# Tiles 6 and 7 turned by moves and VectorE, regrouping by pairs through the DRAM, ScalarE normalising tiles 8 to 15

## The chip, the cores and the metric

The kernel runs on one core of a Trainium2 chip. The metric is the device time in microseconds (us) of one execution; lower is better.

## The reference, cut to what matters

`x` is 2048 tokens of 512 features, all float32. It is layer-normalised to `xn`; a linear-attention block and a two-layer block with a squared ReLU both read `xn`, and their results are added to `x`.

```python
xn  = (x - mean(x)) / sqrt(var(x) + 1e-5)
q, k, v = split(xn @ wqkv)                     # 32 heads of 16
phi = lambda t: where(t > 0, t + 1, exp(t)) + 1e-6
kv  = sum over tokens of phi(k)^T v            # per head
z   = sum over tokens of phi(k)
o   = (phi(q) @ kv) / (phi(q) . z + 1e-6)
out = x + o @ wo + relu(xn @ w1 + b1)**2 @ w2 + b2
```

## The kernel before, in words

The tokens are 16 tiles of 128, in blocks of TB = 4 tiles. Every matrix product is made of float32r products of a high and a low part: ScalarE copies the high part ("high", L292, or `copy`, L108), and VectorE or GpSimd makes the rest ("low", L295, or L116).

The part that matters here is the loop over tiles, L617 to L653. Iteration i, called **step i** below, issues on TensorE `project(i)` (L335, 12 matmuls into the PSUM bank `pk`: the keys of tile i) and `kx(i - 1)` (L354, 12 matmuls that add phi(k)^T xn of the tile before to four banks `kx`). So TensorE alternates 12 `pk` and 12 `kx` matmuls. `project(i)` needs the normalised tile with features on the partitions, in high and low parts. There are two ways to turn a tile:

- **By TensorE** (`turned_pe`, L271), tiles 0 to 7: four transposes (L276) into a bank `pt`; then ScalarE takes the high part, VectorE the low part, both from PSUM, and ScalarE copies the turned tile once more to SBUF (`keep_t`, L297) from where it is stored to DRAM (`xTd`, L302). In step i they turn tile i + 1, between `project(i)` and `kx(i - 1)`.
- **By moves and VectorE** (`turn`, L259), tiles 8 to 15: normalised tiles are written in a permuted order, 16 DMAs of 64 KB per four tiles (`regroup`, L245) move them from SBUF to SBUF so that 32 x 32 blocks stand right, and one VectorE transpose (L261) turns a tile. TensorE has no part in it.

VectorE computes mean and variance (`measure`, L213, L214), ScalarE a first inverse root (`roots`, L224, L225), VectorE refines it (L233 to L235) and normalises (L241). Both stand in step 2 to 7 for the tiles listed in `ahead` (L613): two tiles a step, out of order, (4, 8, 9) first. `phi` is ScalarE relu and exp (L326, L328) and VectorE's L330; `parts` makes the high part of phi(k) on ScalarE (L108) and the low part on VectorE (L343). `tokens` makes high (ScalarE) and low (GpSimd, L116) parts of the tile itself for `kx`. `pieces` (L607) takes the weights for later (`wq`, `wo`, `wv`) through ScalarE and VectorE, two a step from step 8 on; `fetch` loads them, at most three ahead.

The order on each engine is the order in which the program is written; there is no scheduler. All DMAs are issued by SyncE (SP), in order, and an SP instruction that waits holds up all DMAs behind it. [...] `regroup` only puts DMAs on the list `moves`; `move(n)` (L254) issues n of them, 16 a step before step 7 and 8 from then on.

After the loop come the queries, the attention and the two-layer block, twice eight tiles; nothing there is changed, except that `regroup_q` uses the old `regroup` under a new name.

## Time and profile before

| | |
|---|---|
| median of 3 runs | 423.33 us (423.31 to 423.94) |
| the profiled execution's own time | 423.45 us |
| its span in the profile | 421.7 us |
| TensorE matmuls busy | 416.7 us (99%) |
| VectorE, ScalarE, GpSimd busy | 298.4, 249.0, 28.5 us |
| granted TensorE clock | 1.0 |
| the tile loop of steps 3 to 15 on TensorE | 23.17 to 95.82 us of the span |

The span is counted from the first profiled instruction to the last; the execution's own time is 1.75 us more. Times of an instruction are from the span's start. TensorE's matmuls overlap in their pipeline, so the distance of their starts counts and not the length of one. The chain of waits follows the work that ended last backwards; where it lists only TensorE pieces without a gap, TensorE waited for nobody.

### The profile page before, as it was taken

The numbers are of one execution on the slowest core, as the hardware profiler recorded it, in microseconds if no ns is written. First come the engines' busy times: TensorE is split into PE (matmuls) and PEld (weight loads), VectorE is DVE, ScalarE is ACT, GpSimd is POOL, SyncE is SP. The second block draws the span as 40 slices with busy tenths as digits, with TensorE's granted clock in tenths as the row PEclk, the third lists the DMA queues.
The fourth block names the chain that finished last, engine by engine and source line by source line (L and its number), as shares of the span: only waits on it lengthen the run. The fifth ranks groups of instructions, "written<-read, shape, count | busy, mean of one in ns | idle before, by whom it ended". The sixth has DMA issues, their size and how long they took to land.

```text
span 421.7 us, 5377 instructions
## 1 busy us (share of the span) xinstructions
PE 416.7 (99%) x1868; PEld 344.9 (82%) x1868; DVE 298.4 (71%) x538; ACT 249.0 (59%) x445; POOL 28.5 (7%) x50
## 2 busy tenths in 40 slices
PE   8999999999999999999999999999999999999996
PEld 7788888888887888888888888888888888888885
DVE  6897788954678887777579376586977668577253
ACT  5866657645467777566466353666667665556140
POOL 3241222230000000000000000000000000000000
PEclk9999999999999999999999999999999999999999
DMA  7862347000412221546026652501120654024602
GB/s 230 284 186 75 101 108 222 21 0 3 112 50 66 85 87 39 188 88 174 0 64 195 185 201 82 139 0 50 51 75 25 200 100 151 1 89 92 163 0 99
DMA packets 42754, 43.02 MB, mean 102 GB/s; under 512 B 5828, under 2 KB 28612, under 8 KB 42472
## 3 DMA queue, kind: packets, MB, share of 16 engines
q1 hardware_dynamic: 42728, 42.69, 35.0%
q8 instruction: 14, 0.23, 0.2%
q14 instruction: 12, 0.10, 0.1%
HBM read 30.09 MB, written 6.29 MB: 86 GB/s over the span
## 4 chain that ended last, share of the span: by engine, by line
PE 98%; DVE 1%; DMA 1%; ACT 0%; issue 0%
PE acc L127 38%; PE b L427 23%; PE kx L354 10%; PE pk L335 10%; PE pq L335 10%; PE pz L127 1%; PE b L127 1%; PE pkv L737 1%; PE pt L276 1%; DMA x<-in_A_x_dram 1%; PE pm L127 1%; PE end L127 0%; DVE st L213 0%; DVE xp L241 0%; DVE res L867 0%; ACT xs1h L292 0%
## 5 line engine op out<-in xcount | busy, mean ns | idle before, releaser
L127 PE MATMUL acc<-w2r,s 128*128 128x512 f32 x498 | 116.6, 389 | 0.0
L127 PEld LDWEIGHTS acc<-w2r,s 128*128 128x128 f32 x498 | 93.5, 188 | 19.6
L427 PE MATMUL b<-T,aop 128*128 128x512 f32 x240 | 59.6, 389 | 0.0
L427 PEld LDWEIGHTS b<-T,aop 128*128 128x128 f32 x240 | 45.0, 188 | 9.4
L354 PE MATMUL kx<-pk,tok 128*128 128x512 f32 x192 | 47.1, 394 | 0.0
L354 PEld LDWEIGHTS kx<-pk,tok 128*128 128x128 f32 x192 | 35.4, 188 | 7.9 <-DVE pk L343 0.6
L127 PE MATMUL acc<-mh,aTsr 128*128 128x512 f32 x96 | 30.3, 390 | 0.0
L108 ACT ACTIVATE w2r<-r 128x512 fp32r<-128x512 f32 x32 | 20.0, 625 | 13.5 <-PE acc L127 11.0
L119 DVE TENSOR_TENSOR w2r<-r,w2r 128x512 fp32r<-128x512 f32 x32 | 21.9, 685 | 7.3 <-ACT w2r L108 6.4
L427 PE MATMUL b<-xs0h,aop 128*128 128x512 f32 x80 | 26.4, 391 | 0.0
L116 POOL TENSOR_TENSOR tok<-xp,tok 128x512 fp32r<-128x512 f32 x16 | 22.4, 1405 | 53.7 <-ACT tok L108 53.7
L116 DVE TENSOR_TENSOR s<-c,s 128x512 fp32r<-128x512 f32 x20 | 13.8, 692 | 16.7 <-ACT s L108 16.7
L330 DVE SCALAR_TENSOR_TENSOR q<-pq,q 128x512 f32<-128x512 f32 x16 | 11.0, 689 | 17.0 <-ACT q L328 17.0
L108 ACT ACTIVATE aop<-S 128x512 fp32r<-128x512 f32 x20 | 12.6, 629 | 14.6 <-DVE S L666 9.4
L127 PEld LDWEIGHTS acc<-mh,aTsr 128*128 128x128 f32 x96 | 18.0, 188 | 3.8
L198 POOL MEMSET r<- 32x512 f32 x3 | 1.6, 522 | 278.3 <-DVE w2r L119 278.2
L326 ACT ACTIVATE q<-pq 128x512 f32<-128x512 f32 x16 | 9.5, 591 | 18.0 <-PE pq L335 18.0
L867 DVE TENSOR_TENSOR res<-acc,res 128x512 f32<-128x512 f32 x16 | 11.0, 691 | 12.6 <-PE acc L127 12.6
L326 ACT ACTIVATE k<-pk 128x512 f32<-128x512 f32 x16 | 9.5, 595 | 16.9 <-PE pk L335 16.8
L127 PE MATMUL acc<-ml,aTsr 128*128 128x512 f32 x48 | 18.7, 390 | 0.0
L427 PEld LDWEIGHTS b<-xs0h,aop 128*128 128x128 f32 x80 | 15.0, 188 | 3.4 <-ACT rz L415 0.3
L261 DVE STREAM_TRANSPOSE at<-g 128x512 f32<-128x512 f32 x16 | 10.5, 690 | 8.5 <-DMA g<-q 8.5
(187 smaller groups left out, 835.7 us busy)
## 6 DMA issues: line engine op xcount, KB each, us to landing
r<-in_B_w_dram SPq DMA_DIRECT2D x49, 256.0 KB, 3.2
res<-in_A_x_dram SPq DMA_DIRECT2D x8, 512.0 KB, 6.2
g<-q SPq DMA_DIRECT2D x64, 64.0 KB, 2.1
out_dram<-res SPq DMA_DIRECT2D x15, 256.0 KB, 2.1
x<-in_A_x_dram SPq DMA_DIRECT2D x5, 512.0 KB, 6.3
xTd<-t SPq DMA_DIRECT2D x8, 256.0 KB, 3.5
rq<-in_A_wqkv_dram SPq DMA_DIRECT2D x8, 256.0 KB, 6.0
xg<-xp SPq DMA_DIRECT2D x32, 64.0 KB, 2.0
```

The costliest lines, as they stand in the source:

```text
L108: nc.scalar.activation(o, i, AF.Copy, bias=bias)
L116: ENG[el].tensor_tensor(out=l, in0=src, in1=f32(h), op=OP.subtract)
L119: nc.vector.tensor_tensor(out=l, in0=src, in1=f32(h), op=OP.subtract)
L127: nc.tensor.matmul(ps, lhsT=a[u], rhs=b[v], start=first and n == 0, stop=last and n == 2)
L261: nc.vector.transpose(o.rearrange("p j (r t) -> p r j t", r=NJ), G.rearrange("p r (j c) -> p r j c", j=NJ))
L276: nc.tensor.transpose(t[k][:, at:at + P], xp[i][:, j * P:(j + 1) * P], ident)
L326: nc.scalar.activation(p, ps, AF.Relu, scale=-1.0)
L330: nc.vector.scalar_tensor_tensor(p, ps, 0.0, p, op0=OP.max, op1=OP.add)
L335: nc.tensor.matmul(ps, lhsT=cols(i)[u][:, j, slot(i)], rhs=w[v][:, j, :], start=first and n == 0, stop=last and n == len(steps) - 1)
L354: nc.tensor.matmul(kxp[c], lhsT=tok[i][:, u, c * P:(c + 1) * P], rhs=pk[i][:, v], start=i == 0 and (u, v) == first, stop=i == NT - 1 and ( ...
L427: nc.tensor.matmul(ps, lhsT=a[u][:, j * P:(j + 1) * P], rhs=b[v][:, j, :], start=first and j == 0 and n == 0, stop=last and j == 1 and n == 2,
L867: nc.vector.tensor_tensor(out=r[:, a:z], in0=ps, in1=r[:, a:z], op=OP.add)
```

## The change

`NDVE` = 6 is the first tile that is turned by moves and VectorE, instead of `NPE` = 8, which stays the first tile whose turned form is kept in SBUF. Tiles 6 and 7 are still normalised by VectorE and still stored to `xTd`, from the buffer that VectorE's transpose writes. Tiles 8 to 15 are normalised by ScalarE: one ACTIVATE with a scale and a bias of one number per partition, after one more tiny VectorE operation on the statistics.

`regroup` now works on a pair of tiles, (6, 7), (8, 9), ... (14, 15): one DMA writes the pair (512 KB) to a DRAM tile `via`, and four DMAs of 128 KB read it back regrouped. The four are issued by `move()`, which now stands at the head of each step.

The order of the steps changes too. Tiles 4, 6, 7 are measured first and normalised in step 2, tile 5 in step 3, and the pairs (8, 9), (10, 11), (12, 13), (14, 15) in steps 4, 6, 8 and 10, on ScalarE behind `tokens`. One tile is measured in each of steps 2 to 9. Tiles 6 to 12 are turned at the end of step i - 2; tiles 13, 14 and 15 at the head of the VectorE work of step i - 2. The weight pieces stand in steps 11 to 13 (two a step) and 14 and 15 (three a step).

```diff
     def normalise(tiles, st, mv, y):
...
+        if tiles[-1] >= NPE:
+            nc.vector.scalar_tensor_tensor(u, mv[:, :n, 0], -1.0, r, op0=OP.mult, op1=OP.mult)
+        later = []
+        def last(i, o, src, k):
+            nc.scalar.activation(o, src, AF.Identity, bias=u[:, k:k + 1], scale=r[:, k:k + 1])
+            if i in groups:
+                regroup(i)
...
+    def regroup(i):
+        src, G = groups[i]
+        via = dram.tile([P, NJ, src.shape[-1]], F32, name=f"via{i}")
+        nc.sync.dma_start(via, src)
+        of_g = via.rearrange("(r t) g n -> g t r n", r=NJ)
+        for g in range(NJ):
+            moves.append((G[32 * g:32 * (g + 1)], of_g[g]))
...
     def transposed(i, n=1):
...
-        if i < NPE:
+        if i < NDVE:
             t = turned_pe(i, n)
         else:
-            t = [xT[b][:, :, at]]
+            t = [xT[b][:, :, at] if i >= NPE else w512(f"t{i}", "p", 6).rearrange("p (j t) -> p j t", j=NJ)]
             turn(t[0], xg[i])
...
-    ahead = {3: (5, 10), 4: (6, 11), 5: (7, 12), 6: (13, 14), 7: (15,)}
...
+        move()
         fetch()
...
-        if i + 1 < NPE:
+        if i + 1 < NDVE:
             high, low, keep_t = transposed(i + 1)
-        k = NPE if i + 1 == NPE else i + 2
-        turned = transposed(k) if i + 1 >= NPE and k < NT else ()
+        soon_turned = transposed(i + 2) if 11 <= i and i + 2 < NT else ()
...
         phi_k(i, ps, high, late)
-        run(*turned)
-        if soon:
-            normalise(*soon)
+        run(*soon_turned)
+        later = normalise(*soon) if soon else []
         parts(i)
         keep_t()
...
-        if i + 1 == NPE:
-            run(*transposed(NPE + 1))
-        pieces(2 if i >= NPE else 0)
-        soon = statistics(*ahead[i + 1]) if i + 1 in ahead else ()
-        move(8 if i >= NPE - 1 else 16)
+        run(*later)
+        if NDVE <= i + 2 < 13:
+            run(*transposed(i + 2))
+        pieces(0 if i < 11 else 2 if i < 14 else 3)
+        if i == 2:
+            ahead[3] = statistics(5)
+        if i + 2 in (4, 6, 8, 10):
+            ahead[i + 2] = group(i + 6, i + 7)
+        if i < 10:
+            measure(ahead[(i + 2) // 2 * 2], i % 2)
+        soon = ahead.get(i + 1, ())
         kx(i - 1)
```

More of the change, by code (lines that the diff above doesn't have):

```diff
@@ L60 @@
     NPE = 2 * TB
+    NDVE = NPE - 2
     WARM = 11
@@ L235, in normalise, with regroup_here @@
         nc.vector.scalar_tensor_tensor(r, u, 1.5, y0, op0=OP.add, op1=OP.mult)
+        if tiles[-1] >= NPE:
[5 more added lines that the diff above has]
+                regroup(i)
         for k, i in enumerate(tiles):
             o, src = xp[i], xr[i]
-            if i >= NPE:
+            if i >= NDVE:
                 o, src = o.rearrange("p g (j c) -> p g j c", j=NJ), gjc(src)
-            nc.vector.tensor_scalar(o, src, mv[:, k, 0:1], r[:, k:k + 1], op0=OP.subtract, op1=OP.mult)
-            if i in groups:
-                regroup(*groups[i])
-    def regroup(src, G):
+            if i < NPE:
+                nc.vector.tensor_scalar(o, src, mv[:, k, 0:1], r[:, k:k + 1], op0=OP.subtract, op1=OP.mult)
+                if i in groups:
+                    regroup(i)
+            else:
+                later.append(lambda a=(i, o, src, k): last(*a))
+        return later
+    moves = []
+    def regroup(i):
[5 more added lines that the diff above has]
+            moves.append((G[32 * g:32 * (g + 1)], of_g[g]))
+    def regroup_here(src, G):
         for r in range(NJ):
@@ L250, in regroup @@
         return G
-    moves = []
     def move(n=8):
@@ L297, in keep_t @@
         def keep_t():
-            if i < NPE:
+            o = t[0]
+            if i < NDVE:
                 o = w512(f"t{i}", "p", 6).rearrange("p (j t) -> p j t", j=NJ)
@@ L301, in keep_t @@
                     copy("act", o[:, k * m:(k + 1) * m], t[k])
+            if i < NPE:
                 nc.sync.dma_start(xTd[b][:, :, at], o)
@@ L310, in ones @@
     def ones(i):
-        nc.gpsimd.memset(xp[i][:, D - 1:] if i < NPE else xp[i][:, NJ - 1, P - 1:], 1.0)
+        nc.gpsimd.memset(xp[i][:, D - 1:] if i < NDVE else xp[i][:, NJ - 1, P - 1:], 1.0)
     def tokens(i):
@@ L317, in tokens @@
         src = xp[i]
-        if i >= NPE:
+        if i >= NDVE:
             h, l, src = gjc(h), gjc(l), src.rearrange("p g (j c) -> p g j c", j=NJ)
         split(h, l, src, "act", "pool")
-        if NPE <= i + 1 < NT:
+        if NDVE <= i + 1 < NT:
             ones(i + 1)
@@ L383, in regroup_q @@
     def regroup_q(b):
-        Gs[b] = regroup(q[b].rearrange("p i (g c) -> p g i c", g=NJ),
+        Gs[b] = regroup_here(q[b].rearrange("p i (g c) -> p g i c", g=NJ),
                         four(f"g{b}", {3: "r1", 2: "r2", 1: "r0", 0: "r3"}[b]).rearrange("p i (r c) -> p r i c", r=NJ))
@@ L471 @@
         a = first_xp[i0]
-        if i0 < NPE:
-            for k in range(TB):
-                xp[i0 + k] = a[:, k]
-        else:
-            o = four(f"xg{i0}", "r0" if i0 + TB == NT else "r3")
-            a, o = (t.rearrange("p a (g c) -> p (a g c)", g=NJ) for t in (a, o))
-            groups[i0 + TB - 1] = [t.rearrange("p (g n) -> p g n", g=NJ) for t in (a, o)]
-            a, o = (t.rearrange("p (g i c) -> p g i c", g=NJ, i=TB) for t in (a, o))
-            for k in range(TB):
-                xp[i0 + k], xg[i0 + k] = a[:, :, k], o[:, :, k]
+        for k in range(TB):
+            xp[i0 + k] = a[:, k]
+        if i0 + TB <= NDVE:
+            continue
+        n = TB if i0 >= NPE else NPE - NDVE
+        o = work.tile([P, n, 512], F32, name=f"xg{i0}", tag="r0" if i0 + TB == NT else "r3" if i0 >= NPE else "rc")
+        for k in range(0, n, 2):
+            i = i0 + TB - n + k
+            u, v = (t.rearrange("p a (g c) -> p (a g c)", g=NJ) for t in (a[:, TB - n + k:][:, :2], o[:, k:k + 2]))
+            groups[i + 1] = [t.rearrange("p (g n) -> p g n", g=NJ) for t in (u, v)]
+            u, v = (t.rearrange("p (g i c) -> p g i c", g=NJ, i=2) for t in (u, v))
+            for m in range(2):
+                xp[i + m], xg[i + m] = u[:, :, m], v[:, :, m]
     def heads_k(*js, eng="act"):
@@ L552 @@
     project(2, pks[2], wk, HL)
-    soon = group(4, 8, 9)
+    soon = group(4, 6, 7)
     phi_k(0, pks[0])
@@ L611, in pieces @@
             fetch()
-    ahead = {3: (5, 10), 4: (6, 11), 5: (7, 12), 6: (13, 14), 7: (15,)}
+    ahead = {}
     kxp = [bank(f"kx{c}", "acc") for c in range(NJ)]
```

## The prediction

> **What bounds the kernel now.** I read the page's busy row first, then the chain of waits, then who TensorE waited for.

> ```profile
> span 421.7 us, 5377 instructions
> PE 416.7 (99%) x1868; PEld 344.9 (82%) x1868; DVE 298.4 (71%) x538; ACT 249.0 (59%) x445; POOL 28.5 (7%) x50
> ```

> TensorE is busy for all but 5.0 us of the span. So the time can only fall by work that TensorE loses, and it can rise by any wait that TensorE gains.

> ```profile
> PE pt L276 <- DVE y L233: 0.6, 1, 0.6
> PE pk L335 <- ACT xs1h L292: 0.3, 1, 0.3
> ```

> ```profile
> 6.38 0.08 DVE y L233
> ...
> 6.98 0.39 ACT xs1h L292
> ...
> 37.74 0.44 PE pt L276 x4
> 38.18 2.77 PE kx L354 x12
> 40.95 2.72 PE pk L335 x12
> 43.67 0.44 PE pt L276 x4
> 44.11 2.75 PE kx L354 x12
> 46.86 2.72 PE pk L335 x12
> 49.58 2.72 PE kx L354 x12
> 52.30 2.72 PE pk L335 x12
> ...
> 65.90 2.72 PE kx L354 x12
> ...
> 82.22 2.72 PE kx L354 x12
> ```

> The first two rows are TensorE's only waits for the result of another engine; the chain has them at 6.38 and 6.98 us, where nothing is changed. From 37.74 on the rows of the chain follow each other without a gap:  the transposes of tile 6 (37.74), the products of tile 4 (`kx`) and of tile 6 (`pk`, 40.95), the transposes of tile 7 (43.67), and so on. A product group takes 2.72 us. Later groups of the chain are known by counting on, 5.44 us a step: 65.90 is where `project(10)` has ended, 82.22 where `kx(12)` starts.

> **What the change removes from TensorE.** Eight transposes. From the end of `project(5)` to the end of the next `kx` is 40.95 - 37.74 = 3.21 us, and 46.86 - 43.67 = 3.19 us one step on; without a transpose it is 52.30 - 49.58 = 2.72 us. So 0.49 + 0.47 = **0.96 us** goes, if nothing is late in its place. Everything else in the change is on the other engines, and is worth nothing or costs a wait. From here on, a place that was at t in the trace is due at t - 0.96, once both tiles are past.

> **What it adds, moves, and how late each may be.** The durations:

> ```profile
> L241 DVE TENSOR_SCALAR xp<-x,mv,y 128x512 f32<-128x512 f32 x16 | 9.2, 605 | 0.4
> L261 DVE STREAM_TRANSPOSE xT<-xg 128x512 f32<-128x512 f32 x8 | 5.6, 702 | 0.5 <-issue 0.5
> L330 DVE SCALAR_TENSOR_TENSOR k<-pk,k 128x512 f32<-128x512 f32 x16 | 10.8, 678 | 6.5 <-ACT k L328 6.3
> L326 ACT ACTIVATE k<-pk 128x512 f32<-128x512 f32 x16 | 9.5, 595 | 16.9 <-PE pk L335 16.8
> L328 ACT ACTIVATE k<-k 128x512 f32<-128x512 f32 x16 | 10.1, 633 | 0.3
> L108 ACT ACTIVATE pk<-k 128x512 fp32r<-128x512 f32 x16 | 10.1, 631 | 4.7 <-DVE k L330 4.7
> L108 ACT ACTIVATE tok<-xp 128x512 fp32r<-128x512 f32 x16 | 9.8, 618 | 0.0
> L292 ACT ACTIVATE xs1h<-xT 128x512 fp32r<-128x512 f32 x4 | 2.5, 629 | 4.2 <-DVE xT L261 4.2
> L409 ACT ACTIVATE c<-c 128x512 f32<-128x512 f32 x20 | 12.5, 625 | 0.3
> L415 ACT ACTIVATE c<-c,b1s 128x512 f32<-128x512 f32 x10 | 7.2, 725 | 8.9 <-DVE c L891 8.9
> ```

> *ScalarE normalising.* No row shows an ACTIVATE with a scale and a bias per partition. L409 (neither) takes 0.625 us and L415 (a bias) 0.725, so one such operand costs 0.10 us. I take 0.825 for two, bounded by 0.725 below and twice that, 1.45, above. That is 8 x 0.825 = 6.6 us more on ScalarE, less two copies of `pt`; VectorE loses 8 x 0.605 and gains 2 x 0.702 and four tiny operations, about 3 us less.

> In a step that normalises a pair, ScalarE's chain from the end of `project(i)` is relu 0.595, exp 0.633, VectorE's k 0.678 (the tiny `roots` run beside it), the high part of phi(k) 0.631, the token copy 0.618, two normalisings 1.65, the high part of the next turned tile 0.629: 5.43 us. A step is 5.44 us, so ScalarE is just free when the next project ends, and the step after has only 3.78 us of it. The high part of tile i + 2 is due three groups, 8.16 us, after `project(i)` ended, so it has 2.7 us to spare; at 1.45 us each the two normalisings would use 1.25 of these. Covered.

> *The way of a pair through the DRAM.* These rows bound it:

> ```profile
> xTd<-t SPq DMA_DIRECT2D x8, 256.0 KB, 3.5
> xt<-xTd SPq DMA_DIRECT2D x2, 1024.0 KB, 4.8
> x<-in_A_x_dram SPq DMA_DIRECT2D x5, 512.0 KB, 6.3
> xg<-xp SPq DMA_DIRECT2D x32, 64.0 KB, 2.0
> ```

> ```profile
> L257 SPq DMA_DIRECT2D xg<-xp x32: 513/588/606, 36.1 to 65.2; - x32
> ```

> The write of 512 KB lies between 3.5 us (256 KB stored) and 6.3 us (512 KB in a full queue); 1 MB in a quiet queue took 4.8, so I take 4.0. The reads wait on SP for the write to land; the fourth is issued 3 x 0.588 = 1.77 us after the first and lands 2.0 (64 KB) to 3.5 us (256 KB) later; I take 2.3. So 4.0 + 1.77 + 2.3 = **8.1 us** from the last normalising to a pair that can be turned, between 7.3 and 11.6.

> [...]

> When may the way end? For pairs up to (12, 13), VectorE turns tile i + 2 at the end of step i. The pair left ScalarE at 5.43 - 0.63 = 4.80 us after `project(i - 2)` ended, and two steps are 10.88 us; the turn must be done 0.629 before the 8.16 us are over. That leaves 10.88 + 8.16 - 0.629 - 0.702 - 4.80 = 12.9 us, more than 11.6. For tiles 6 and 7:

> ```profile
> 23.50 1.46 DVE L241 TENSOR_SCALAR xp<-x,mv,y 128x512 f32<-128x512 f32 x3
> 35.69 0.68 DVE L343 SCALAR_TENSOR_TENSOR pk<-k,pk 128x512 fp32r<-128x512 f32 x1
> ```

> The three normalisings of step 2 end at 24.96 (now tiles 4, 6, 7). The turn of tile 6 stands behind the second row, at 36.4, and `project(6)` is due at 40.95 - 0.49 = 40.46, so the pair may land until 39.1: 14.2 us. DMAs queued behind this write on SP (the store of tile 3, `b1s`) are wanted by nobody soon.

> **Tile 14 is the tight one**: it is turned at the head of step 12's VectorE work, with k(12), the low parts and everything later queued behind it. Its pair leaves ScalarE at 65.90 - 0.96 + 4.80 = 69.7, and lands at 77.8. `kx(12)` is due at 82.22 - 0.96 = 81.26 and needs the turn (0.702), k (0.678) and the high part (0.631) first, so 79.25 is the latest: 9.5 us after the issue. It holds by 1.4 us on my value.

> *Queues moved past.* The reads now stand on SP ahead of the fourth `wq` load, which so is issued near 76.1 (69.7 + 4.0 + 4 x 0.588) and is used at 81 (77.8, then 0.702, 0.678, 0.631, 0.618 and a piece of about 0.62). At the 6.3 us of the x row it would come 1.4 us late, with relu(13) behind it on ScalarE; `kx(13)` is due 5.44 us after `kx(12)` and hides that, since relu to the high part of phi(k) takes 2.5 of the 5.44 us that follow `project(13)`. The weight pieces move from steps 8 to 13 to steps 11 to 15; the last ones (wv) fall where the trace has VectorE waiting:

> ```profile
> 99.87 0.69 DVE L330 SCALAR_TENSOR_TENSOR q<-pq,q 128x512 f32<-128x512 f32 x1 [3.30 <-ACT q L328]
> ```

> Three pieces of 0.69 us fit into these 3.3 us of idle time, which end at 99.87 where the queries start. In steps 14 and 15 no tile is turned, which pays for the third piece.

> *The low parts of tiles 6 and 7* now come from SBUF, beside GpSimd's token operation:

> ```profile
> 59.63 1.34 POOL L116 TENSOR_TENSOR tok<-xp,tok 128x512 fp32r<-128x512 f32 x1 [5.35 <-ACT tok L108]
> 60.17 1.94 DVE L116 TENSOR_TENSOR wql<-rq,wqh 128x512 fp32r<-128x512 f32 x2 [0.36 <-ACT wqh L108]
> ```

> Two VectorE operations of about 0.69 us took 1.94 us beside GpSimd's 1.34. I charge 0.6 us to such a low part; it is due later than the high part, which has 2.7 us.

> [...]

> **The sum.** 423.45 (the profiled execution: span 421.7 and 1.75 around it) - 0.96 = 422.49. The median of the runs is 0.12 below that execution, so 423.33 - 0.96 = **422.4 us**.

> **The rivals.**

> 1. *The way through the DRAM is late for tile 14* (slower than before). VectorE stands at the turn, k(12) behind it, TensorE waits before `kx(12)`. From 9.5 us on each microsecond costs one; from 10.5 the gain is gone; from 11.3 it is slower by over 0.2%. At the upper bound of 11.6 the stall is 2.1 us: 422.4 + 2.1 = 424.5. For it: a write and reads in series, the 6.3 us row. Against: that row is from the first 25 us with a full queue, while at 70 us only this pair and two weight loads are on the way.
> 2. *Half is given back* in small waits: a low part behind GpSimd (0.6), ScalarE full in steps 4 to 10 (5.43 of 5.44). One wait of about 0.5 us: 422.9. Against: each has over a microsecond to spare.
> 3. *The transposes go, but no time*: TensorE then waits for the same moment of another engine. 423.3. Against: no group after 8 us waited for anyone, and VectorE gets lighter.

> **How the numbers follow.** Forecast 0.60, rival 1 0.15 (half of it past the 0.2% mark, the rest inside), rival 2 0.17, rival 3 0.08. A change of about 0.2% (0.85 us) is what a measurement of this kernel can tell from none, and 0.96 is only just beyond it, so 0.06 of the forecast may fall inside. Faster by over 0.2%: 0.60 - 0.06 = 0.54. Slower: half of rival 1, and as much again, taken from rival 2, for a stall larger than I see, 0.15. Same: the remaining 0.31. The range goes from 422.1 (a quarter of a microsecond for the scatter and the early waits) to 424.0 (rival 1 with a way of 11.1 us), which leaves out less than 2 in 10.

> **What would show it.** In the profile after: no `pt` group between 37 and 47 us, `project(7)` at 45.9 instead of 46.86, and `kx(12)` at 81.3. `via` to last landing within 9.5 us, and the transposes of tiles 6 to 15 without a DMA named in their idle time. A normalising ACTIVATE of 0.73 to 0.9 us. Wrong would be a TensorE wait on `kx` or `pk` for VectorE or ScalarE after 20 us, or a transpose of tile 14 that waits for a DMA past 79.

## The result and the profile after

The changed kernel takes **422.51 us** (median of 13 runs, 422.31 to 422.84), the kernel before 423.40 us (13 runs, 423.24 to 423.94): 0.89 us less, a ratio of 0.9979 with a 95% interval of 0.997 to 0.9987 (0.55 to 1.27 us). The prediction was 422.4. The profiled execution took 422.49 us.

The head of its page, then whom TensorE waited for (total, times, longest):

```profile
span 420.8 us, 5373 instructions
PE 415.2 (99%) x1860; PEld 343.6 (82%) x1860; DVE 294.2 (70%) x536; ACT 254.0 (60%) x451; POOL 27.6 (7%) x50
```

```profile
PE pt L300 <- DVE y L234: 1.1, 1, 1.1
...
PE pk L361 <- ACT xs1h L316: 0.3, 1, 0.3
```

Eight matmuls fewer, 1868 to 1860, are the transposes. TensorE's waits are still those of the first microseconds. The chain of waits (start, length) passes over the place of the change without a gap:

```profile
23.07 2.73 PE pk L361 x12
...
34.92 2.72 PE pk L361 x12
37.64 2.72 PE kx L380 x12
40.36 2.72 PE pk L361 x12
43.08 2.72 PE kx L380 x12
45.80 2.72 PE pk L361 x12
...
81.16 2.72 PE kx L380 x12
...
94.76 5.44 PE pq L361 x24
```

No `pt` stands between 37 and 47 us. `project(7)` is at 45.80, `kx(12)` at 81.16, as forecast (45.9 and 81.3). The queries begin at 94.76 instead of 95.82: 1.06 us, of which 0.10 arose before the loop reaches the changed tiles (`project(3)` at 23.07 instead of 23.17).

What the other engines do, by groups (count, busy us and mean ns, idle time ahead of them and its cause):

```profile
L243 ACT ACTIVATE xp<-x,y 128x512 f32<-128x512 f32 x8 | 6.0, 802 | 0.0
L285 DVE STREAM_TRANSPOSE xT<-xg 128x512 f32<-128x512 f32 x8 | 5.6, 705 | 2.0 <-DMA xg<-via 2.0
L285 DVE STREAM_TRANSPOSE t<-xg 128x512 f32<-128x512 f32 x2 | 1.4, 704 | 0.0
L319 DVE TENSOR_TENSOR xs0l<-t,xs0h 128x512 fp32r<-128x512 f32 x2 | 1.4, 693 | 2.3 <-ACT xs0h L316 2.3
```

Only one turn waits for a DMA, tile 14's. Its way: the DMAs of the last pair on SP, the turn on VectorE, and the spread from issue to landing of all reads:

```profile
69.49 0.34 SPq L266 DMA_DIRECT2D via<-xp  x1
72.13 1.73 SPq L281 DMA_DIRECT2D xg<-via  x4
73.90 0.43 SPq L162 DMA_DIRECT2D rq<-in_A_wqkv_dram  x1
74.38 2.73 SPq L162 DMA_DIRECT2D ro<-in_A_wo_dram  x4
```

```profile
78.11 0.71 DVE L285 STREAM_TRANSPOSE xT<-xg 128x512 f32<-128x512 f32 x1 [2.05 <-DMA xg<-via]
```

```profile
DMA to landing us min/median/max: 2.6/3.0/4.5
```

The write is issued at 69.49, the first read 2.64 us later, and the turn begins at 78.11: 8.62 us for the whole way. VectorE stood for 2.05 us; TensorE did not notice.

### The profile page after: what moved, and what is told of

It is laid out like the page before. It is cut to its first block, busy times and chain, and to the rows that moved or that the text cites. A ratio compares the mean times of both kernels' runs of the same rounds, so it can differ in the third digit from the quotient of the medians.

```text
span 420.8 us, 5373 instructions
## 1 busy us (share of the span) xinstructions
PE 415.2 (99%) x1860; PEld 343.6 (82%) x1860; DVE 294.2 (70%) x536; ACT 254.0 (60%) x451; POOL 27.6 (7%) x50
## 4 chain that ended last, share of the span: by engine, by line
PE 98%; DVE 1%; DMA 1%; ACT 0%; issue 0%
PE acc L128 39%; PE b L453 23%; PE kx L380 10%; PE pk L361 10%; PE pq L361 10%; PE pz L128 1%; PE b L128 1%; PE pkv L773 1%; PE pm L128 1%; DMA x<-in_A_x_dram 1%; PE pt L300 1%; PE end L128 0%; DVE st L214 0%; DVE xp L253 0%; DVE res L903 0%; ACT xs1h L316 0%
## 5 line engine op out<-in xcount | busy, mean ns | idle before, releaser
L109 ACT ACTIVATE w2r<-r 128x512 fp32r<-128x512 f32 x32 | 20.0, 625 | 13.8 <-PE acc L128 11.3
L903 DVE TENSOR_TENSOR res<-acc,res 128x512 f32<-128x512 f32 x16 | 11.0, 692 | 14.2 <-PE acc L128 14.2
L453 PE MATMUL b<-xs0l,aop 128*128 128x512 f32 x40 | 15.6, 389 | 0.0
L285 DVE STREAM_TRANSPOSE at<-g 128x512 f32<-128x512 f32 x16 | 10.5, 689 | 6.8 <-DMA g<-q 6.8
## 6 DMA issues: line engine op xcount, KB each, us to landing
r<-in_B_w_dram SPq DMA_DIRECT2D x49, 256.0 KB, 3.2
res<-in_A_x_dram SPq DMA_DIRECT2D x8, 512.0 KB, 5.9
out_dram<-res SPq DMA_DIRECT2D x15, 256.0 KB, 2.1
x<-in_A_x_dram SPq DMA_DIRECT2D x5, 512.0 KB, 5.6
via<-xp SPq DMA_DIRECT2D x5, 512.0 KB, 2.6
xTd<-t SPq DMA_DIRECT2D x8, 256.0 KB, 3.1
```

The source lines that it names most:

```text
L109: nc.scalar.activation(o, i, AF.Copy, bias=bias)
L285: nc.vector.transpose(o.rearrange("p j (r t) -> p r j t", r=NJ), G.rearrange("p r (j c) -> p r j c", j=NJ))
L453: nc.tensor.matmul(ps, lhsT=a[u][:, j * P:(j + 1) * P], rhs=b[v][:, j, :], start=first and j == 0 and n == 0, stop=last and j == 1 and n == 2,
L903: nc.vector.tensor_tensor(out=r[:, a:z], in0=ps, in1=r[:, a:z], op=OP.add)
```

## The experiments

Theory: the gain is the 0.96 us of the eight transposes; all the rest is covered, tile 14's pair most tightly. Rivals: the gain comes from elsewhere (lighter VectorE, statistics one a step); or the cover is not what I named.

### 1 and 2: where the gain comes from

After, with tiles 6 and 7 turned by TensorE again:

```diff
-    NDVE = NPE - 2
+    NDVE = NPE
```

> The changed kernel with tiles 6 and 7 turned by TensorE again; pairs through the DRAM, ScalarE's normalising, the order of the statistics and of the weight pieces stay. If the gain is the eight transposes alone, it is all given back: 0.0 us against the kernel before (within 0.2), 423.4 us. If the gain comes from the lighter VectorE or the new order, it stays: 422.5 us.

423.41 us (11 runs, 423.12 to 423.97), ratio to before 0.9998 (0.9989 to 1.0006). The chain has the two groups again:

```profile
37.62 0.44 PE pt L300 x4
...
43.55 0.44 PE pt L300 x4
```

Everything else of the change is in this kernel, and without the turns it brings nothing. In its profiled execution (423.60 us) `kx(12)` also takes 3.00 instead of 2.72 us, and tile 14 was turned only at 80.02: not all that this one execution is longer is the transposes.

The other way round: before, without the transposes of tiles 6 and 7. `project` reads the tiles unturned, so the keys of these two tiles are not the reference's:

```diff
+        if i in (6, 7):
+            ones(i)
+            return [xp[i].rearrange("p (j t) -> p j t", j=NJ)]
```

> The kernel before without the eight transposes of tiles 6 and 7; their products read the normalised tile as it is, not turned, so this part of the computation is left out, and nothing else is changed. If TensorE is the bound, it is 0.96 us faster than the kernel before: 422.45 us. If another engine sets the pace of steps 5 to 8, less than half of that.

422.47 us (12 runs, 422.16 to 424.26), ratio 0.9976 (0.9967 to 0.9985), 1.0 us less than 423.47. The profiled execution is the longest of the twelve, 424.26 us, for a reason of its own (last section), so the median of the runs is what counts here. So the eight transposes alone are worth what the whole change brings, and nothing else of it is needed to explain the gain.

### 3 and 4: is ScalarE's normalising needed?

After, with VectorE normalising tiles 8 to 15 again, ahead of `parts`:

```diff
-        if tiles[-1] >= NPE:
+        if False:
...
-            if i < NPE:
+            if True:
```

> The changed kernel with VectorE normalising tiles 8 to 15 as it did before, ahead of the low part of phi(k). VectorE gets 4 x 1.1 us more in steps 4, 6, 8 and 10, where the trace of the changed kernel shows it idle for 1 us or more a step. If only the transposes count, the time stays 422.5 us (within 0.2). If moving the normalising to ScalarE is part of the gain, it comes to 422.8 to 423.4 us.

423.41 us (11 runs, 422.74 to 423.84), ratio 0.9993 (0.9984 to 1.0001): the 422.5 us that I would have if only the transposes counted is missed, the gain is gone. First VectorE and GpSimd around step 10 of this kernel, then the chain:

```profile
68.79 1.00 DVE L253 TENSOR_SCALAR xp<-x,mv,y 128x512 f32<-128x512 f32 x2
69.71 1.78 DVE L369 SCALAR_TENSOR_TENSOR pk<-k,pk 128x512 fp32r<-128x512 f32 x1
```

```profile
69.44 1.50 POOL L117 TENSOR_TENSOR tok<-xp,tok 128x512 fp32r<-128x512 f32 x1 [3.48 <-ACT tok L109]
```

```profile
69.80 1.71 DVE pk L369
...
71.55 1.89 PE kx L380 x7
73.44 2.73 PE pk L361 x12
```

VectorE's same operation in the changed kernel, where GpSimd's begins at 68.13:

```profile
67.62 0.69 DVE L369 SCALAR_TENSOR_TENSOR pk<-k,pk 128x512 fp32r<-128x512 f32 x1
```

VectorE is late here already (it makes k(10) at 67.51 instead of 66.17), and with 1.00 us of normalising on top the low part of phi(k) falls beside GpSimd's token operation and takes 1.78 instead of 0.69 us. `kx(10)` waits for it in the middle of its matmuls, and `project(12)`, which follows, starts at 73.44 instead of 73.00: 0.44 us.

To try that reason, the same kernel with the products that use this low part put last in `kx`:

```diff
-        order = (((1, 0),), ((0, 0), (0, 1))) if i >= NPE else (((0, 0),), ((0, 1),), ((1, 0),))
+        order = (((1, 0),), ((0, 0),), ((0, 1),)) if i >= NPE else (((0, 0),), ((0, 1),), ((1, 0),))
```

> The third experiment (VectorE normalises tiles 8 to 15) with one more edit: from tile 8 on, the four products of kx that use the low part of phi(k) come last, behind the four with its high part, where they were taken by turns. Theory A (VectorE's low part of phi(k), held for 1.79 us beside GpSimd's token operation, is what costs the third experiment its 0.9 us): the low part is then wanted 4 x 0.227 us later than now, which is more than the stall of 0.44 us in kx(10), so no stall is left and the time is 422.4 to 422.7. Theory B (the loss sits elsewhere: in the pieces, the turns, or the end): 423.2 to 423.6 stays.

423.14 us (11 runs, 422.77 to 423.61), ratio 0.9991 (0.9982 to 1.0). Theory A's number is missed, and theory B's 423.2 lies inside the scatter: the low part is at most a part of the loss. The chain, and TensorE's weight loads:

```profile
70.38 2.72 PE kx L380 x12
73.09 2.88 PE pk L361 x12
```

```profile
72.94 0.19 PEld L361 LDWEIGHTS pk<-wkh,xs0h 128*128 128x128 f32 x1 [0.26 <-ACT xs0h L316]
```

`kx(10)` runs through, so the late low part was the stall of 0.44 us. But the turn of tile 12 stands behind that operation on VectorE, and its high part is now what `project(12)` waits for: it takes 2.88 instead of 2.72 us. The rest lies mostly outside the span, where no row shows it. Over the runs, the median time outside the span is 1.71 us in the changed kernel, 2.08 in experiment 3 and 2.11 in experiment 4. So of the 0.90 us of experiment 3, 0.37 lies outside the span and 0.44 is the stall; of the 0.63 us of experiment 4, 0.40 lies outside and 0.3 in the span, half of it `project(12)`. Why these two have 0.4 us more there stays open: the kernel before, where VectorE normalises all tiles, has not, and experiment 5, where ScalarE normalises, has 1.91 us. So the stall shows that ScalarE's normalising keeps 0.44 us; the other 0.4 us go with it, without a cause that is shown.

### 5: without the DRAM

After, with 16 moves of 32 KB per pair from SBUF to SBUF in place of one write and four reads:

```diff
     def regroup(i):
+        regroup_here(*groups[i])
...
-        move()
+        move(16)
```

> The changed kernel with the pairs regrouped from SBUF to SBUF by 16 DMAs of 32 KB each, not through the DRAM. The sixteenth is issued 9 us after the pair (14, 15) is normalised at 69.5 and lands 2 us later, at 80.5 to 82, while the latest for tile 14 is 79.1 (81.16 less 2.01). If that limit is real, TensorE stalls ahead of kx(12) by 1.4 to 3 us: 423.9 to 425.5 us, slower than the kernel before. If VectorE's order leaves more room than I count, it stays at 422.5 us.

431.96 us (4 runs), ratio 1.019 (1.0172 to 1.0208): slower as expected, by far more. SP's queue and TensorE's longest wait:

```profile
51.48 33.44 SPq L276 DMA_DIRECT2D xg<-xp  x48
```

```profile
PE kx L375 <- ACT pk L109: 2.9, 1, 2.9
```

48 issues take 33.44 us, 0.70 each, so a pair keeps SP busy for 11.1 us, about the two steps (10.88 us) that it has. The pairs queue up, and the last one lands at 86.2 instead of 78.1. TensorE waits 2.1 us for a pair at 53.5 us and 2.9 us for the last one, and is granted half its clock for 3.4 us behind each (0.59 from 88 to 92 us, 0.992 over the span), which is worth 1.7 us each (see the next experiment): together 8.4 of the 9.4 us. The way through the DRAM takes SP five issues instead of sixteen, 2.07 us for the last pair of the changed kernel (0.34 and 1.73) instead of 11.1; that is what it is good for.

### 6, 7 and 8: what lateness of the last pair costs

After, with one more copy, DRAM to DRAM, for the pair (14, 15):

```diff
+        if i == NT - 1:
+            first, via = via, dram.tile([P, NJ, src.shape[-1]], F32, name="hop")
+            nc.sync.dma_start(via, first)
```

> The changed kernel with one more copy from DRAM to DRAM (512 KB) between the write and the four reads of the last pair alone, tiles 14 and 15. The pair landed at 78.1 and may be as late as 79.1; a copy takes 2.6 to 4.8 us, so it lands at 80.7 to 82.9. If each microsecond past the limit costs one, TensorE stalls 1.6 to 3.8 us ahead of kx(12): 424.1 to 426.3 us. If the limit is wrong, the time stays 422.5 us, or the stall shows at another place.

426.41 us (7 runs, 424.57 to 429.41), ratio 1.007 (1.0046 to 1.0095). Its chain, and TensorE's wait:

```profile
69.34 2.63 DMA via<-xp
...
71.98 3.94 DMA hop<-via
...
77.25 3.36 DMA xg<-hop
...
80.80 0.72 DVE xT L288
...
82.90 4.53 PE kx L383 x12
```

```profile
PE kx L383 <- ACT pk L109: 1.9, 1, 1.9
```

The stall is where it was expected, and `kx(12)` behind it takes 4.53 instead of 2.72 us. The table of one-microsecond windows shows why (behind the window its length, the busy share of TensorE, its weight loads, VectorE, ScalarE and GpSimd; then the granted clock, the DMA engines' share and GB/s):

```profile
84.00:85.00 1.00, 1.00 (x4) 0.81 (x3) 1.00 (x1) 0.97 (x3) 0.72 (x2) 0.50 1.03 395
...
86.00:87.00 1.00, 1.00 (x4) 0.81 (x3) 1.00 (x2) 0.51 (x1) 0.00 (x0) 0.50 0.50 188
87.00:88.00 1.00, 1.00 (x5) 0.78 (x4) 0.88 (x3) 1.00 (x3) 0.00 (x0) 0.80 0.53 162
```

From 84 us on TensorE is granted half its clock for 3.41 us, which costs it half of that, 1.7 us. The price of the stall was 1.9 + 1.8 us. Two shorter stalls, made by writing tile 14 again on ScalarE (the same values) two and three times more:

```diff
-            nc.scalar.activation(o, src, AF.Identity, bias=u[:, k:k + 1], scale=r[:, k:k + 1])
+            for _ in range(3 if i == 14 else 1):
+                nc.scalar.activation(o, src, AF.Identity, bias=u[:, k:k + 1], scale=r[:, k:k + 1])
```

> Two more ACTIVATEs on tile 14 (the same values written again), so the last pair leaves ScalarE 2 x 0.80 = 1.6 us later and lands near 79.7 instead of 78.1, against a latest landing of 79.1: a stall of about 0.6 us before kx(12). Theory A (a stall costs what it lasts): 422.5 + 0.6 = 423.1. Theory B (any stall of this kind also lowers the clock that TensorE is granted for the next groups, as the 1.9 us stall of the second hop did at 1.8 us): 424 to 425, with a granted clock under 0.9 in the microseconds behind the stall.

423.40 us (11 runs, 422.85 to 423.74), ratio 0.9997 (0.9988 to 1.0006). Wait and chain:

```profile
PE kx L381 <- ACT pk L109: 0.7, 1, 0.7
```

```profile
82.03 2.96 PE kx L381 x12
```

The same with one more:

```diff
-            for _ in range(3 if i == 14 else 1):
+            for _ in range(4 if i == 14 else 1):
```

> Three more ACTIVATEs on tile 14: 2.4 us later, landing near 80.5, a stall of about 1.4 us. Theory A (a stall costs what it lasts): 423.9. Theory B (the clock falls for about 3 us behind it): 425 to 426. A third way: the clock stays full behind 0.6 us and falls behind 1.4; then there is a length of stall from which it decides, and these two runs lie on its two sides.

424.55 us (11 runs, 423.88 to 426.02), ratio 1.0026 (1.0015 to 1.0036). Wait, chain, and the window that was at half clock in experiment 6:

```profile
PE kx L381 <- ACT pk L109: 1.6, 1, 1.6
```

```profile
82.89 2.98 PE kx L381 x12
```

```profile
84.00:85.00 1.00, 1.00 (x6) 0.84 (x5) 1.00 (x1) 0.97 (x3) 0.73 (x2) 1.00 1.00 381
```

Stalls of 0.7 and 1.6 us cost their length and 0.25 us more, as `kx(12)` takes 2.96 and 2.98 instead of 2.72 us. (0.16 of this is a matter of counting: the idle time is counted from the end of a matmul of 0.39 us, while the next one otherwise starts 0.23 us after its start.) That gives 422.51 + 0.7 + 0.24 = 423.45 and 422.51 + 1.6 + 0.26 = 424.37, against 423.40 and 424.55. In these two profiled executions the clock stayed at 1.00, so theory B does not hold in them.

For the runs without a profile, the granted clock on average over the span tells it: 3.41 us at half clock lower it by 0.004. Of the seven runs with the second hop, those of 424.57 and 424.84 us have 1.000, the five others 0.996 or 0.992. Of the two runs of 426.0 us with the stall of 1.6 us, one has 0.996 and the other 0.999: the first had such a stretch, the second did not, and why it is 1.5 us longer than the median stays open. So the clock fell behind the stall of about 1.9 us in five of the seven executions. A length from which it falls is not shown; the last section has a case with less idle time.

### 9 and 10: the neighbours of the last pair

After, with the weight pieces from step 8 on, two a step:

```diff
-        pieces(0 if i < 11 else 2 if i < 14 else 3)
+        pieces(2 if i >= NPE else 0)
```

> The changed kernel with the weight pieces where they were before, two a step from step 8 on. VectorE's work of steps 8 and 10 comes to 6.3 us and ScalarE's to 6.4 us, of steps of 5.44 us, and 2 us of lateness gather up to step 10; the parts have 1.5 to 2.9 us to spare. If the moved pieces are needed for the gain, it is 422.8 to 423.5 us; if the slack holds, 422.5 us.

428.32 us (4 runs), ratio 1.0118 (1.0103 to 1.0132): missed by 5 us. SP's queue, the chain and the wait:

```profile
71.04 0.33 SPq L266 DMA_DIRECT2D via<-xp  x1
71.46 0.38 SPq L162 DMA_DIRECT2D ro<-in_A_wo_dram  x1
71.89 0.78 SPq L622 DMA_DIRECT2D wv<-in_A_wqkv_dram  x1
...
74.10 1.91 SPq L281 DMA_DIRECT2D xg<-via  x4
```

```profile
75.57 7.07 DMA xg<-via
...
84.76 4.38 PE kx L380 x12
```

```profile
PE kx L380 <- ACT pk L109: 3.6, 1, 3.6
```

Two things are seen. The pieces push the normalising of the last pair back, so its write is issued at 71.04 instead of 69.49. And the loads that the pieces ask for now stand between the write and the reads; the last read takes 7.07 us to land. How much of the 7.07 us the loads make is not shown, as something else fell into this read too (experiment 10). The stall is 3.6 us, and `kx(12)` takes 1.66 us more behind it, as in the second hop. So the later place of the pieces, which I had passed as harmless, is also what keeps the way free.

Then after with the loads fetched five ahead instead of three:

```diff
-        while todo and len(held) < 3:
+        while todo and len(held) < 5:
```

> The changed kernel with up to five weight loads ahead of their use instead of three, so that most of the loads that follow the last pair's reads (at 73.9 to 77 us) are issued near 20 us. If those loads made the last read of tile 14 land after 4.5 us instead of about 2.8, VectorE's wait of 2.05 us before the turn of tile 14 falls under 1 us, and the time does not change (422.5 us), since the wait was covered. If the loads had nothing to do with it, the wait stays 2 us.

422.55 us (11 runs, 422.45 to 424.15), ratio 0.9981 (0.9973 to 0.999). The turn of tile 14:

```profile
77.84 0.71 DVE L285 STREAM_TRANSPOSE xT<-xg 128x512 f32<-128x512 f32 x1 [1.77 <-DMA xg<-via]
```

It waits 1.77 instead of 2.05 us, nearer to what I expected if the loads had nothing to do with it. Three `ro` loads and one of `wv` still follow the reads, but other runs speak against them as the cause too: in experiments 3 and 4 the reads have `rq` and `ro` loads right behind them, as in the changed kernel, and the third read takes 2.99 and 2.96 us to land instead of 4.52. What differs in the traces is a DMA packet of 16 KB that the profile lists under a queue of its own, "instruction". It comes at 74.86 us in the changed kernel and at 74.42 here, in the middle of the reads, and only at 78.58 and 79.01 us in experiments 3 and 4. In the seven kernels where it falls into the reads (after and experiments 1, 7, 8, 10, 11, 12) their last packet starts 4.35 to 5.62 us after the first read is issued; in the three where it falls outside (3, 4, 6), 3.47 to 3.73. In experiment 9 it came at 80.00, and the last read's packets ended at 82.1. No run moves this packet alone, so that it is the cause is likely and not shown.

The time is the same, as it should be for an engine that nobody waits for. One of the eleven runs took 424.15 us at a granted clock of 1.000; no row says why.

### 11 and 12: a further version

After, with the three product groups of `kx` for tiles 0 to 7 in another order, the low part of phi(k) last:

```diff
-        order = (((1, 0),), ((0, 0), (0, 1))) if i >= NPE else (((0, 0),), ((0, 1),), ((1, 0),))
+        order = (((1, 0),), ((0, 0), (0, 1))) if i >= NPE else (((0, 0),), ((1, 0),), ((0, 1),))
```

> The changed kernel with the products of kx for tiles 0 to 7 in another order: high by high, then the token's low part, then phi(k)'s low part last. In the trace kx(0) takes 2.90 us and kx(1) 2.97 us because phi(k)'s low part comes late behind GpSimd's token operation, whose own result is there in time. If so, both take 2.72 to 2.77 us and the time is 422.1 us, 0.4 us below the changed kernel. If the wait only moves to the token's low part, 422.5 us.

422.35 us (9 runs, 422.24 to 422.92), ratio 0.9976 (0.9967 to 0.9986). In its chain `kx(0)` takes 2.73 us, in the changed kernel 2.90; `kx(1)` is as long as before (3.03 us, 2.97 in the changed kernel), since it is the high part that is late there. That is half of what I expected, and the intervals of the two versions overlap; as a time, the 0.16 us are not shown. With the order of experiment 4 for tiles 8 to 15 as well:

```diff
-        order = (((1, 0),), ((0, 0), (0, 1))) if i >= NPE else (((0, 0),), ((1, 0),), ((0, 1),))
+        order = (((1, 0),), ((0, 0),), ((0, 1),)) if i >= NPE else (((0, 0),), ((1, 0),), ((0, 1),))
```

> The version with the low part of the tokens ahead (tiles 0 to 7), and from tile 8 on the products with phi(k)'s low part last. If no group of kx waits for a low part now, as the chain shows none behind 24 us, the second edit brings nothing: 422.3 to 422.5, as without it. If low parts held beside GpSimd cost a little in some executions, the interval gets narrower and the time is 422.2 to 422.3.

422.46 us (8 runs, 422.34 to 422.66), ratio 0.9975 (0.9965 to 0.9985): no further gain, as no `kx` of these steps waits for a low part.

## Why the prediction was right

*The eight transposes, 0.96 us.* Right, and shown from both sides: with them back the gain is gone (experiment 1), and taken from the kernel before they give 1.0 us (experiment 2). From 23.07 to 94.76 the tile loop is 71.69 us against 72.65 in the profiled executions, the 0.96 us that were forecast. This also settles rivals 2 and 3: no small wait gave any of it back. That the medians differ by 0.21%, just beyond the mark of 0.2%, is luck: the interval goes from 0.13 to 0.30%.

*ScalarE's normalising.* 0.825 us was taken, 0.802 measured. The chain of a pair step just fits, as costed. But "everything else in the change ... is worth nothing or costs a wait" holds only as long as the change is taken whole: with the normalising left on VectorE, the turns of tiles 6 and 7 bring nothing (experiment 3). It is a cover of the gain, which the prediction did not name; 0.44 of the 0.9 us is explained by a wait, the rest is not.

*The low parts of tiles 6 and 7*, charged 0.6 us each behind GpSimd: they take 0.693 us, beside nothing. A low part that took longer beside GpSimd was seen, but another one in another kernel: that of phi(k) in experiment 3, 1.78 instead of 0.69 us beside 1.50 us of GpSimd. Why it takes longer there is not shown.

*The way through the DRAM*, 8.1 us: 8.62 measured, by errors that nearly cancel, which is luck. The write took 2.64 us up to the first read instead of 4.0 (it lies below my lower bound, 3.5, which came from the row of the 256 KB stores), and the fourth read was issued 1.30 us after the first instead of 1.77. The last read then took over 4 us to land instead of 2.3, also beyond the bound of 3.5; what makes it slow is hardly the weight loads behind it and more likely a packet of the instruction queue (experiment 10), which the prediction did not count. One sign that was forecast did not come: the turn of tile 14 does wait for a DMA, for 2.05 us up to 78.11, still ahead of the 79 us that would have been wrong.

*The latest landing for tile 14*, 79.25: right. Experiments 7 and 8 turned it at 79.93 and 80.80 and stalled for 0.7 and 1.6 us, which puts it at 79.2. The slack was 1.1 us, not 1.4, and in experiment 1's trace it is used up (80.02, where the transposes put the latest at about 80.1).

*The price in rival 1*, "from 9.5 us on each microsecond costs one": this is the mis-sized step. Stalls of 0.7 and 1.6 us cost their length and 0.25 us; behind one of 1.9 us the clock mostly costs 1.8 more. The rival's 424.5 for a stall of 2.1 us would have been over 426, an estimate from experiment 6.

*The weight pieces*: they fit. The three of `wv` run from 95.43 for 1.89 us, and VectorE still waits 1.50 us behind them where it waited 3.30. That they had to leave steps 8 to 10 was not seen (experiment 9).

## What to carry to other kernels

Where one engine is busy throughout, as TensorE is here (99% of the span), the gain of a change is the work that it takes from that engine (0.96 us of transposes, 0.89 us of time), and the rest of the change is to be read as what keeps the others out of its way. Such a part can look worthless in the trace and yet be needed: undo it alone to see. Its size alone did not set the time of a transfer here: the third read of 128 KB took 3.0 us for most pairs and 4.5 for the last one, where a packet of the instruction queue fell into the reads, and three weight loads stood ahead of the read of 7.07 us. So leave slack for what the program itself does not order.

## What the runs showed of the hardware that was not expected

```profile
6.56 0.63 PE L279 MATMUL pt<-ident,xp 128*128 128x128 f32 x4 [1.34 <-DVE y L233]
```

```profile
8.00:9.00 1.00, 1.00 (x6) 1.00 (x5) 0.55 (x1) 0.38 (x3) 0.00 (x0) 0.50 0.95 180
```

That execution took 424.26 us, 1.8 us more than its kernel's median. At the same place experiment 9, with 1.33 and 0.26 us, and the changed kernel, with 1.12 and 0.26 us, kept 1.00. What decides is not shown.

Two kernels in which VectorE normalises tiles 8 to 15 within the new order have 2.08 and 2.11 us outside the span instead of 1.71, experiment 5 has 1.91, and no row of the profile shows where.
